# Softmax and its backward in parts between other steps, and score rows in another order, in an attention-and-FFN backward kernel

## The chip, the cores and the metric

The kernel runs on one core of a Trainium2 chip. The metric is the device time of one execution in microseconds (us). Before the change the median of three runs is 317.88 us (315.27 to 318.63). The profile below is of one more execution, with a span of 321.8 us from its first to its last instruction.

## What is computed

The forward pass is a layer norm, then grouped-query attention for one new token per batch entry plus a gated FFN, added to the input. The kernel returns the output and the gradients of eight inputs.

```python
B, Sq, D = 4, 1, 512;  Hq, Hkv, Sk, Dh = 32, 8, 4096, 128;  F = 1792
def _A_ref(x, k_cache, v_cache, wq, wo):
    W = min(4096, max(256, Sk // 4))              # 1024: only the last W keys are used
    rep = Hq // Hkv                               # 4 query heads for each key head
    q = (x @ wq).reshape(B, Sq, Hq, Dh).transpose(0, 2, 1, 3)
    k = jnp.repeat(k_cache[:, :, Sk - W:, :], rep, axis=1)
    v = jnp.repeat(v_cache[:, :, Sk - W:, :], rep, axis=1)
    p = _softmax(jnp.einsum("bhqd,bhkd->bhqk", q, k) * (Dh ** -0.5), axis=-1)
    o = jnp.einsum("bhqk,bhkd->bhqd", p, v)
    return o.transpose(0, 2, 1, 3).reshape(B, Sq, Hq * Dh) @ wo
def _B_ref(x, w_gate, w_up, w_down):
    return (_gelu(x @ w_gate) * (x @ w_up)) @ w_down
xn = _layernorm(A_x)
out = A_x + _A_ref(xn, A_k_cache, A_v_cache, A_wq, A_wo) + _B_ref(xn, B_w_gate, B_w_up, B_w_down)
# outputs: out and the gradients of A_x, k_cache, v_cache, wq, wo, w_gate, w_up, w_down, all bfloat16
```

The gradients of the two caches have the caches' full size (4 x 8 x 4096 x 128). Keys before the last 1024 take no part, so three quarters of both gradients are zeros, which the kernel writes from one tile of zeros (50 MB).

## The kernel before

The kernel first does the FFN and its backward, then the attention in four groups (t = 0 to 3) of two key heads. Matmuls run on TensorE (PE), evictions from PSUM on ScalarE (ACT) and VectorE (DVE), one masked copy of P, the masks and the stores' issue on GpSimd (POOL), loads on SyncE (SP). The zeros are issued from ACT's queue, at fixed places between its evictions.

Work that only feeds stores stands in a list `bg` of small pieces: one matmul and one eviction each; the last piece of a tile issues its store. `tick(n)` places the next n of them.

```python
    def tick(n):
        for _ in range(min(n, len(bg))):
            bg.popleft()()

    def scores(t, k):                     # k = 0: S = Q K^T;  k = 1: dP = dO V^T
        ...
        for g in range(GP):               # GP = 2 key heads
            for q in range(NQ):           # NQ = 4 quarters of the keys: 8 steps in all
                T_ps = ps_w.tile([P, JQ, P], BF16, name="T_ps", tag="w")
                for jj in range(JQ):      # 8 transposes
                    nc.tensor.transpose(T_ps[:, jj, :], blks[(t, g)][:, q * JQ + jj, :], ident[:])
                T_sb = tsb.tile([P, WQ, B], BF16, name="T_sb", tag="T", bufs=4)
                evac(T_sb..., T_ps..., 1024, half=True)              # on DVE
                for b in range(B):
                    nc.tensor.matmul(ps[b * RG:(b + 1) * RG, :], lhsT=..., rhs=T_sb[:, :, b], ...)
                tick(2)
                if q == 1:
                    zeros(4 if (g, k) != (0, 0) else 2 if t == NT - 1 else 0)

    def transposed(src, nm):
        pT_ps = ps_w.tile([P, JQ, P], BF16, name="pT_ps", tag="w")
        for jj in range(JQ):
            nc.tensor.transpose(pT_ps[:, jj, :], src[:, jj, :], ident[:])
        pT = attw.tile([P, JQ, P], BF16, name=nm, tag=nm, bufs=1)
        evac(pT[:].rearrange("p j (h b) -> p j b h", b=B),           # written in another order: PT, dST
             pT_ps[:].rearrange("p j (b h) -> p j b h", b=B), 1024, half=True)
        return pT[:].rearrange("p j (q g r) -> p j q g r", q=NQ, g=GP)

    def softmax(t):
        ...   # DVE: row maximum m;  PE: its transpose mT;  DVE: maximum over the quarters, negated
        ...   # PE: back to a column nm;  DVE: negm;  ACT: E_f = exp(S + negm), row sums es
        ...   # PE: es_ps, sums over the quarters;  DVE: rr = 1 / sum;  ACT: P_b = E_f * rr
        P_x = by_batch(P_b, "P_x", nc.gpsimd)                        # POOL: P spread by batch entry
        st[t].update(E=E_f, rr=rr, PT=transposed(P_x, "PT"), P=P_x)

    def softmax_d(t):
        ...   # DVE: gs = row sums of E_f * dP;  PE: gs_ps;  DVE: cc, Gt = (dP - cc) * E_f, dS_b
        dS_x = by_batch(dS_b, "dS_x", nc.vector)
        st[t].update(dST=transposed(dS_x, "dST"), dS=dS_x)

    def odq(t):                           # o from P^T and V, dq from dS^T and K
        for j in range(J):                # J = 32; four matmuls each, 16 rows of weights
            ...
                    nc.tensor.matmul(od_ps[r0:r0 + rep * B, :], lhsT=pT[:, j % JQ, j // JQ, g],
                                     rhs=blks[(t, g)][:, j, :], ...)
        ...   # od_r (DVE), its transpose od_T, and od_x, a masked copy on POOL

    # the pieces, each with its store through POOL:
    # dvdk(t, 0), dvdk(t, 1): 16 each (kv_ps; P_x or dS_x against the masks domr, qmr), 2 stores of 1 MB
    # dw(t): 8 dwo_ps and 8 dwq_ps from od_x, 4 stores of 0.5 MB (osb_o, osb_q; three buffers)

    # FFN backward: 14 iterations of transposes, eviction, matmuls, and tick(1)

        for t in range(NT):
            if t == 0:
                pre(t)                    # do and q of the group: woT steps, then wq; tick(2) a woT step
            masks(t)
            scores(t, 0)
            zeros(2 if t == 0 else 0)
            softmax(t)
            dvdk(t, 0)
            scores(t, 1)
            softmax_d(t)
            dvdk(t, 1)
            zeros(2 if t >= NT - 2 else 0)
            if t + 1 < NT:
                pre(t + 1)
            odq(t)
            fin(t)                        # sums for out and dx; four wqT steps with tick(2)
            load_next(t)                  # loads of group t + 2 into the buffers of group t
            dw(t)
        tick(len(bg))
        zeros(2 * B * G)                  # what is left of the zeros
```

The order in which the instructions of the loop stand on each engine is settled by a scheduler when the kernel is built; each engine then runs its own list in order.

Of the kernel before, what the change touches and what calls it, by code (L numbers as in the profile page):

```python
# [14 lines left out]
P = 128  # L15
# [3 lines left out]
def kernel(  # L19
# [94 lines left out]
    for eng, dst, src in ((nc.sync, dy_b, grad_out), (nc.scalar, x_b, A_x)):  # L114
# [18 lines left out]
    hmsk_f = const.tile([P, GP, rep * B], FP32, name="hmsk_f")  # L133
    idv = ident_f[:].rearrange("p (k g x) -> p k g x", k=2, g=GP)[:, :, :, 0:rep * B]
    nc.vector.tensor_tensor(out=hmsk_f[:], in0=idv[:, 0], in1=idv[:, 1], op=ALU.add)
    hmsk1 = const.tile([P, HG], FP32, name="hmsk1")
    nc.vector.reduce_sum(out=hmsk1[:], in_=hmsk_f[:].rearrange("p g (i b) -> p (g i) b", b=B), axis=AX.X)
    hmsk = const.tile([P, HG], BF16, name="hmsk")
    nc.vector.tensor_copy(out=hmsk[:], in_=hmsk1[:])
# [6 lines left out]
    rsum1 = const.tile([P, B, HG], FP32, name="rsum1")  # L146
    nc.vector.reduce_sum(out=rsum1[:].rearrange("p b h -> p (b h)"),
                         in_=ident_f[:].rearrange("p (b q h) -> p b h q", b=B, q=NQ), axis=AX.X)
    rsum = const.tile([P, B, NQ, HG], FP32, name="rsum")
    nc.vector.tensor_copy(out=rsum[:], in_=rsum1[:].unsqueeze(2).broadcast_to([P, B, NQ, HG]))  # L150

    msk_f = const.tile([P, GP, NQ], FP32, name="msk_f")
    nc.gpsimd.memset(msk_f[:], 1.0)
    for b in range(B):
        rs = slice(b * RG, (b + 1) * RG)
        nc.gpsimd.affine_select(out=msk_f[rs], in_=msk_f[rs], pattern=[[-rep, GP], [-HG, NQ]],
                                compare_op=ALU.is_ge, fill=0.0, base=0, channel_multiplier=1)
        nc.gpsimd.affine_select(out=msk_f[rs], in_=msk_f[rs], pattern=[[rep, GP], [HG, NQ]],
                                compare_op=ALU.is_ge, fill=0.0, base=rep - 1, channel_multiplier=-1)
    msk = const.tile([P, GP, NQ], BF16, name="msk")  # L160
    nc.vector.tensor_copy(out=msk[:], in_=msk_f[:])
# [12 lines left out]
    qm, dom = [const.tile([P, B, NS, RG + rep], BF16, name=nm) for nm in ("qm", "dom")]  # L174
# [56 lines left out]
    for dst, src, own, other in ((dyz, dy_b, slice(0, HP), slice(HP, P)), (xnz, xn_b, slice(HP, P), slice(0, HP))):  # L231
        nc.vector.tensor_copy(out=dst[own, :], in_=src[own, :])
        nc.vector.memset(dst[other, :], 0.0)
# [61 lines left out]
    def pre(t):  # L295

        wo_sb, wq_sb = wo_t[t], wq_t[t]
        dq_ps = ps_x.tile([P, 2, HG, B], FP32, name="doq_ps", tag="x")
        for h2 in range(HG // 2):
# [6 lines left out]
            for i in range(2):  # L306
                for c in range(ND):
                    nc.tensor.matmul(dq_ps[:, 0, 2 * h2 + i, :], lhsT=woT[:, i, c, :], rhs=dyT[:, c, :],
                                     start=(c == 0), stop=(c == ND - 1))
            tick(2)  # L310
        for h in range(HG):
            for c in range(ND):
                nc.tensor.matmul(dq_ps[:, 1, h, :], lhsT=wq_sb[:, c, h * Dh:(h + 1) * Dh], rhs=xnT[:, c, :],
                                 start=(c == 0), stop=(c == ND - 1))
        T4 = []
        for k, (sc, zt, nm) in enumerate(((None, dom, "do"), (scale, qm, "qs"))):
            xT4 = attw.tile([P, B, NQ, HG], BF16, name=nm + "T4", tag=nm + "T4")
            src = dq_ps[:, k].rearrange("p h b -> p b h").unsqueeze(2).broadcast_to([P, B, NQ, HG])
            if sc is None:
                nc.vector.tensor_copy(out=xT4[:], in_=src)  # L320
            else:
                nc.scalar.activation(out=xT4[:], in_=src, func=ACT.Copy, scale=sc)
            nc.vector.tensor_copy(out=zt[:, :, :, 0:rep].rearrange("p b s i -> p (b s) i"),
                                  in_=xT4[:].rearrange("p b q (g i) -> p (b q g) i", i=rep))
            T4.append(xT4)
        r_ps = ps_x.tile([P, 2, P], BF16, name="r_ps", tag="x")
        for k in range(2):
            nc.tensor.transpose(r_ps[:, k, :], T4[k][:].rearrange("p b q h -> p (b q h)"), ident[:])
# [4 lines left out]
    def masks(t):  # L333
        for k, nm in enumerate(("do", "q")):
            mr = attw.tile([P, GP, NQ, Dh], BF16, name=nm + "mr", tag=nm + "mr", bufs=1)
            nc.gpsimd.tensor_tensor(out=mr[:].rearrange("p g q d -> p (g q) d"),
                                    in0=st[t]["r4"][:, k, :].unsqueeze(1).broadcast_to([P, NS, Dh]),
                                    in1=msk[:].rearrange("p g q -> p (g q)").unsqueeze(2).broadcast_to([P, NS, Dh]),
                                    op=ALU.mult)
            st[t][nm] = mr  # L340

    def scores(t, k):

        lf = (qm, dom)[k][:].rearrange("p b s c -> p b (s c)")
        blks = (k_t, v_t)[k]
        ps = ps_a.tile([P, WQ], FP32, name="S_ps", tag=("S", "dP")[k])
        for g in range(GP):
            for q in range(NQ):
# [10 lines left out]
                tick(2)  # L359
# [12 lines left out]
    rsum_f = rsum[:].rearrange("p b q h -> p (b q h)")  # L372

    def transposed(src, nm):
# [5 lines left out]
        evac(pT[:].rearrange("p j (h b) -> p j b h", b=B), pT_ps[:].rearrange("p j (b h) -> p j b h", b=B), 1024, half=True)  # L380
        return pT[:].rearrange("p j (q g r) -> p j q g r", q=NQ, g=GP)

    def softmax(t):
        S = st[t]["S"]
        m = attw.tile([P, 1], FP32, name="m", tag="m")
        nc.vector.reduce_max(out=m[:], in_=S, axis=AX.X)
        mT_ps = ps_x.tile([1, P], FP32, name="mT_ps", tag="x")
        nc.tensor.transpose(mT_ps[:], m[:], ident_f[:])
        mx = attw.tile([1, B, HG], FP32, name="mx", tag="mx")
        nc.vector.reduce_max(out=mx[:].rearrange("o b h -> o (b h)"),  # L390
                             in_=mT_ps[:].rearrange("o (b q h) -> o b h q", b=B, q=NQ), axis=AX.X)
        mx4 = attw.tile([1, B, NQ, HG], FP32, name="mx4", tag="mx4")
        nc.vector.tensor_scalar(out=mx4[:], in0=mx[:].unsqueeze(2).broadcast_to([1, B, NQ, HG]), scalar1=-1.0,
                                scalar2=None, op0=ALU.mult)
        nm_ps = ps_x.tile([P, 1], FP32, name="nm_ps", tag="x")
        nc.tensor.matmul(nm_ps[:], lhsT=mx4[:].rearrange("o b q h -> o (b q h)"), rhs=one_f[:], start=True, stop=True)
        negm = attw.tile([P, 1], FP32, name="negm", tag="negm")
        nc.vector.tensor_copy(out=negm[:], in_=nm_ps[:])
        E_f = attw.tile([P, WQ], FP32, name="E_f", tag="E_f", bufs=1)
        es = attw.tile([P, 1], FP32, name="es", tag="es")  # L400
        nc.scalar.activation(out=E_f[:], in_=S, func=ACT.Exp, bias=negm[:, 0:1], scale=1.0, accum_out=es[:])
        es_ps = ps_x.tile([P, 1], FP32, name="es_ps", tag="x")
        nc.tensor.matmul(es_ps[:], lhsT=rsum_f, rhs=es[:], start=True, stop=True)
        rr = attw.tile([P, 1], FP32, name="rr", tag="rr")
        nc.vector.reciprocal(out=rr[:], in_=es_ps[:])
        P_b = attw.tile([P, WQ], BF16, name="P_b", tag="P_b", bufs=1)
        nc.scalar.activation(out=P_b[:], in_=E_f[:], func=ACT.Copy, scale=rr[:, 0:1])
        P_x = by_batch(P_b, "P_x", nc.gpsimd)
        st[t].update(E=E_f, rr=rr, PT=transposed(P_x, "PT"), P=P_x)

    def softmax_d(t):
        E_f, rr, dP = st[t]["E"], st[t]["rr"], st[t]["dP"]
# [346 lines left out]
```

## Time and profile before

| | before |
|---|---|
| median of three runs | 317.88 us |
| span of the profiled execution | 321.8 us |
| PE busy | 227.2 us (71%) |
| DVE busy | 169.5 us (53%) |
| ACT busy | 115.8 us (36%) |
| POOL busy | 67.7 us (21%) |
| moved by DMA | 112.38 MB (read 30.93 MB, written 81.01 MB) |

The busy time of an engine is the time in which it executes instructions, matmuls as the profile models their ends. "The span in 40 slices" gives the busy share of each engine in equal slices of 8.05 us, in tenths; PEclk is the clock granted to PE, in tenths of full speed, and DMA the mean busy share of the 16 DMA engines. In groups of instructions, a line gives the line of the code, engine, operation, output and input, count, then busy us and mean ns of one, then the idle time of the engine ahead of it and what ended most of that.

### The profile page before, as it was taken

What the parts mean: (1) busy time and instruction counts of PE and PEld (TensorE: products, weight loads), DVE (VectorE), ACT (ScalarE), POOL (GpSimd) and SP (SyncE); (2) the same over time, 40 slices, a digit from 0 to 9 for tenths busy, and PEclk for the clock granted to TensorE, in tenths of its full rate; (3) what the DMA queues carried; (4) which work ended last, traced back from release to release, by engine and by line L of the source; (5) the groups of instructions that cost most, each with busy time, mean ns of one, the idle gap of its engine ahead of it and who ended that gap; (6) DMA issues with size and microseconds to landing.
All of it is one profiled execution on the core that took longest, in us unless ns stands there. A gap on an engine that the chain in (4) does not pass through costs nothing.

```text
span 321.8 us, 6824 instructions
## 1 busy us (share of the span) xinstructions
PE 227.2 (71%) x2954; PEld 151.5 (47%) x2954; DVE 169.5 (53%) x312; ACT 115.8 (36%) x219; POOL 67.7 (21%) x80
## 2 busy tenths in 40 slices
PE   0769986938759894857499938647898487378710
PEld 0768863534437652534376514325664344354210
DVE  7763763526465573534546627263576254626760
ACT  2007752433423464214044622421455244017610
POOL 8200226130001433110033330000413300030400
PEclk9966997765967999577697978696899559558965
DMA  6999999999995799999639999999639969952895
GB/s 238 402 384 413 414 288 423 415 429 432 425 428 233 236 370 429 428 423 427 256 132 323 379 431 425 425 429 395 261 139 370 395 257 399 433 239 117 316 390 224
DMA packets 22013, 112.38 MB, mean 349 GB/s; under 512 B 1560, under 2 KB 7712, under 8 KB 13792
## 3 DMA queue, kind: packets, MB, share of 16 engines
q10 hardware_dynamic: 4624, 50.46, 37.3%
q1 hardware_dynamic: 11600, 30.81, 25.3%
q0 software_dynamic: 5760, 30.67, 24.3%
q8 instruction: 23, 0.38, 0.5%
q14 instruction: 6, 0.05, 0.0%
HBM read 30.93 MB, written 81.01 MB: 348 GB/s over the span
## 4 chain that ended last, share of the span: by engine, by line
PE 47%; DMA 23%; DVE 16%; issue 5%; ACT 4%; POOL 2%; ACTq 1%; SPq 0%; DVEq 0%; POOLq 0%
DMA out_dram<-osb_o 14%; PE kv_ps L461 9%; PE T_ps L351 8%; PE S_ps L356 4%; PE od_ps L434 4%; DMA out_dram<-osb_d 3%; PE wqT_ps L521 3%; DVE dST L96 3%; DMA out_dram<-osb_g 3%; DMA wd_sb<-in_B_w_down_dram 3%; PE acc_ps L196 3%; PE wgT_ps L656 2%; PE woT_ps L303 2%; DVE T_sb L96 2%; PE pT_ps L378 2%
## 5 line engine op out<-in xcount | busy, mean ns | idle before, releaser
L96 DVE COPY T_sb<-T_ps 128x1024 bf16<-128x1024 bf16 x64 | 44.3, 692 | 41.3 <-PE T_ps L351 41.0
L94 ACT CAST stg_dv<-kv_ps 128x512 bf16<-128x512 f32 x53 | 29.2, 588 | 67.6 <-PE kv_ps L461 67.1
L351 PE MATMUL T_ps<-ident,vb 128*128 128x128 bf16 x256 | 30.1, 273 | 7.9 <-DVE PT L96 3.3
L351 PEld LDWEIGHTS <-vb 128*128 128x128 bf16 x256 | 23.5, 125 | 21.3 <-issue 19.8
L94 ACT CAST stg_dk<-kv_ps 128x512 bf16<-128x512 f32 x46 | 25.3, 589 | 19.1 <-PE kv_ps L461 16.4
L461 PE MATMUL kv_ps<-domr,P_x 128*128 128x512 bf16 x64 | 25.7, 472 | 1.1 <-DVE wqT L96 1.1
L94 ACT CAST osb_q<-dwq_ps 128x512 bf16<-128x512 f32 x24 | 13.1, 590 | 36.0 <-PE dwq_ps L493 20.4
L351 PEld LDWEIGHTS <-kb 128*128 128x128 bf16 x256 | 18.6, 102 | 14.5 <-issue 9.2
L351 PE MATMUL T_ps<-ident,kb 128*128 128x128 bf16 x256 | 24.8, 228 | 0.5 <-ACT stg_dk L94 0.4
L461 PE MATMUL kv_ps<-qmr,dS_x 128*128 128x512 bf16 x64 | 21.1, 405 | 0.4
L94 ACT CAST osb_g<-dwg_ps 128x512 bf16<-128x512 f32 (+1 forms) x26 | 13.2, 557 | 21.6 <-PE dwg_ps L632 14.0
L446 POOL TENSOR_TENSOR od_x<-od_r,hmsk 128x1024 bf16<-128x1024 bf16 x4 | 7.5, 1882 | 54.3 <-DVE od_r L438 54.3
L96 DVE COPY PT<-pT_ps 128x1024 bf16<-128x1024 bf16 x4 | 9.7, 2434 | 14.9 <-PE pT_ps L378 14.9
L303 PE MATMUL woT_ps<-ident,wo_sb 128*128 128x128 bf16 x128 | 12.9, 252 | 5.8 <-DVE dST L96 5.8
L356 PE MATMUL S_ps<-T_sb,dom 128*32 128x256 bf16 x128 | 12.8, 390 | 6.0 <-DVE T_sb L96 5.8
L94 ACT CAST osb_o<-dwo_ps 128x512 bf16<-128x512 f32 x25 | 13.6, 588 | 8.7 <-PE dwo_ps L480 8.6
L96 DVE COPY woT<-woT_ps 128x1024 bf16<-128x1024 bf16 x16 | 11.1, 693 | 10.0 <-PE woT_ps L303 10.0
L96 DVE COPY wqT<-wqT_ps 128x1024 bf16<-128x1024 bf16 x16 | 11.0, 689 | 7.1 <-PE wqT_ps L521 7.1
L434 PE MATMUL od_ps<-kb,dST 128*16 128x128 bf16 x256 | 12.8, 281 | 2.5 <-DVE dST L96 2.5
L303 PEld LDWEIGHTS <-wo_sb 128*128 128x128 bf16 x128 | 10.3, 114 | 8.7 <-issue 7.9
L100 POOL DMA_DIRECT2D out_dram<-osb_q x8 | 5.8, 731 | 40.6 <-ACT osb_q L94 27.0
L356 PE MATMUL S_ps<-T_sb,qm 128*32 128x256 bf16 x128 | 12.7, 387 | 2.3 <-DVE T_sb L96 2.2
(194 smaller groups left out, 438.1 us busy)
## 6 DMA issues: line engine op xcount, KB each, us to landing
out_dram<-ztile ACTq DMA_DIRECT2D x8, 3072.0 KB, 16.0
out_dram<-ztile ACTq DMA_DIRECT2D x16, 1536.0 KB, 14.6
kb<-in_A_k_cache_dram SPq DMA_DIRECT2D x8, 1024.0 KB, 14.7
vb<-in_A_v_cache_dram SPq DMA_DIRECT2D x8, 1024.0 KB, 23.1
out_dram<-stg_dv POOLq DMA_DIRECT2D x8, 1024.0 KB, 5.9
out_dram<-stg_dk POOLq DMA_DIRECT2D x8, 1024.0 KB, 8.6
wo_sb<-in_A_wo_dram SPq DMA_DIRECT2D x4, 1024.0 KB, 6.8
wq_sb<-in_A_wq_dram SPq DMA_DIRECT2D x4, 1024.0 KB, 5.8
```

The lines of the kernel that those rows point to most:

```text
L94: last.append(nc.scalar.copy(out=out, in_=in_))
L96: return nc.vector.tensor_copy(out=out, in_=in_)
L196: nc.tensor.matmul(ps[:, c, :], lhsT=lf(c), rhs=rhs, start=(k == 0), stop=(k == len(terms) - 1))
L303: nc.tensor.transpose(wT_ps[:, i, c, :], wo_sb[:, 2 * h2 + i, c * P:(c + 1) * P], ident[:])
L351: nc.tensor.transpose(T_ps[:, jj, :], blks[(t, g)][:, q * JQ + jj, :], ident[:])
L356: nc.tensor.matmul(ps[b * RG:(b + 1) * RG, :], lhsT=lf[:, b, s * RG:(s + 1) * RG], rhs=T_sb[:, :, b], start=(g == 0 and q == 0), stop=(g = ...
L378: nc.tensor.transpose(pT_ps[:, jj, :], src[:, jj, :], ident[:])
L434: nc.tensor.matmul(od_ps[r0:r0 + rep * B, :], lhsT=pT[:, j % JQ, j // JQ, g], rhs=blks[(t, g)][:, j, :], start=(j == 0), stop=(j == J - 1) ...
L446: nc.gpsimd.tensor_tensor(out=X[:], in0=rows[:].unsqueeze(1).broadcast_to([P, HG, Dh]), in1=hmsk[:].unsqueeze(2).broadcast_to([P, HG, Dh]) ...
L461: nc.tensor.matmul(mps[:].rearrange("p q d -> p (q d)"), lhsT=src[:, jj, :], rhs=mr[:, g].rearrange("p q d -> p (q d)"), start=True, stop= ...
L521: nc.tensor.transpose(wT_ps[:, i, c, :], wq_sb[:, c, h * Dh:(h + 1) * Dh], ident[:])
L656: nc.tensor.transpose(wT_ps[:, i, c, :], wsb[:, c, fc * P:(fc + 1) * P], ident[:])
```

## The change

Three things are done.

1. A row of the scores was (batch, quarter, head) and becomes (batch, head in its key head, quarter, key head). The masks, the sums over quarters and the operands of the score matmuls follow. P^T and dS^T can then be copied from PSUM as they stand; the matmuls of `odq` pick their columns with a step of 8. The rows of `dyz` and `xnz` have to be put in the new order too, once, by a matmul with a selection matrix.
2. The softmax is cut into four parts, which are placed after steps 0, 1, 2 and 5 of the dP scores. Its backward is cut in two, placed after woT steps 0 and 2 of the next group's `pre`. The serial chains are meant to run beside other work of PE.
3. The background pieces are spread anew to fit: dV pieces begin within the dP scores, dK pieces within `pre`, all are placed before dW pieces are added, and the FFN backward takes two pieces an iteration instead of one.

```diff
-    def scores(t, k):
+    def scores(t, k, hooks):
 ...
-                tick(2)
+                for f in hooks.get(g * NQ + q, ()):
+                    f()
+                tick(2 if k or q % 2 else 1)
 ...
     def transposed(src, nm):
 ...
-        evac(pT[:].rearrange("p j (h b) -> p j b h", b=B), pT_ps[:].rearrange("p j (b h) -> p j b h", b=B), 1024, half=True)
-        return pT[:].rearrange("p j (q g r) -> p j q g r", q=NQ, g=GP)
+        evac(pT[:].rearrange("p j r -> p (j r)"), pT_ps[:].rearrange("p j r -> p (j r)"), 1024, half=True)
+        return pT
 ...
     def softmax(t):
         m = ...                                   # row maximum, at once
+        def a():  ...                             # mT, maximum over the quarters, mx4
+        def b():  ...                             # nm, negm, E_f and es
+        def c():  ...                             # es_ps, rr, P_b, P_x on POOL; then dvdk(t, 0)
+        def d():  u["PT"] = transposed(u["P"], "PT")
+        return {0: [a], 1: [b], 2: [c], 5: [d]}
 
     def softmax_d(t):
         Gt, gs = ...                              # row sums of E_f * dP, at once
+        def a():  ...                             # gs_ps, cc, Gt, dS_b, dS_x; then dvdk(t, 1)
+        def b():  u["dST"] = transposed(u["dS"], "dST")
+        return a, b
 ...
-                    nc.tensor.matmul(od_ps[r0:r0 + rep * B, :], lhsT=pT[:, j % JQ, j // JQ, g],
+                    nc.tensor.matmul(od_ps[r0:r0 + rep * B, :], lhsT=pT[:, j % JQ, (j // JQ) * GP + g:P:NS],
 ...
-            nc.gpsimd.tensor_tensor(out=mr[:]..., in0=r4 for 8 (g, q), in1=msk, op=ALU.mult)
+            for g in range(GP):
+                nc.gpsimd.tensor_tensor(out=mr[:, g], in0=r4 for 4 q, in1=msk[:, :, g]..., op=ALU.mult)
 ...
     def pre(t, hooks):                            # within the woT steps h2
-            tick(2)
+            for f in hooks.get(h2, ()):
+                f()
+            tick(3 if hooks else 2)
 ...
-        nc.vector.tensor_copy(out=dst[own, :], in_=src[own, :])          # dyz, xnz
+        nc.tensor.matmul(z_ps[own, :], lhsT=sel...[:, own], rhs=src[:], start=True, stop=True, ...)
+        nc.vector.tensor_copy(out=dst[own, :], in_=z_ps[own, :])
 ...
-            tick(1)                               # FFN backward
+            tick(2)
 ...
-            softmax(t)
-            dvdk(t, 0)
-            scores(t, 1)
-            softmax_d(t)
-            dvdk(t, 1)
+            scores(t, 1, softmax(t))
+            d1, d2 = softmax_d(t)
             zeros(2 if t >= NT - 2 else 0)
             if t + 1 < NT:
-                pre(t + 1)
+                pre(t + 1, {0: [d1], 2: [d2]})
+            else:
+                tick(2)
+                d1()
+                tick(6)
+                d2()
+                tick(2)
             odq(t)
             fin(t)
             load_next(t)
+            tick(len(bg))
             dw(t)
```

## The prediction

> **What bounds the kernel now.** I read the page first: the span in 40 slices and the DMA queues.
>
> ```profile
> PEclk9966997765967999577697978696899559558965
> DMA  6999999999995799999639999999639969952895
> GB/s 238 402 384 413 414 288 423 415 429 432 425 428 233 236 370 429 428 423 427 256 132 323 379 431 425 425 429 395 261 139 370 395 257 399 433 239 117 316 390 224
> ...
> q10 hardware_dynamic: 4624, 50.46, 37.3%
> q1 hardware_dynamic: 11600, 30.81, 25.3%
> q0 software_dynamic: 5760, 30.67, 24.3%
> ```
>
> Queue 10 carries the zeros, 1 the loads, 0 the stores. With 0.5% of instruction traffic the shares sum to 87.4% of 321.8 us, so 281 us of transfers: no order of the work goes below that without moving fewer bytes, and the change moves the same bytes. What can be won is the time in which the DMA engines have nothing to do. The digits show it: four dips (slices 12-13, 19-20, 28-29, 35-36), one for each of the four groups, plus the start, a small one at slice 32 and the tail.
>
> Next the stretches around these dips (columns: length; busy us and instructions of PE, PEld, DVE, ACT, POOL; granted PE clock; DMA share; GB/s):
>
> ```profile
> 96.00:104.00 8.00, 7.75 (x161) 5.86 (x164) 4.43 (x9) 2.52 (x5) 0.57 (x1) 0.71 0.54 228
> 104.00:112.00 8.00, 7.06 (x178) 5.32 (x163) 3.98 (x8) 3.64 (x7) 3.76 (x3) 1.00 0.75 251
> 152.00:156.00 4.00, 0.62 (x8) 0.51 (x9) 3.18 (x5) 0.00 (x0) 0.00 (x0) 0.91 0.99 419
> 156.00:168.00 12.00, 9.84 (x232) 7.46 (x232) 5.26 (x8) 3.91 (x7) 2.63 (x3) 0.75 0.31 127
> 220.00:240.00 20.00, 18.70 (x364) 13.75 (x352) 10.37 (x22) 9.10 (x17) 5.46 (x5) 0.83 0.57 234
> 256.00:264.00 8.00, 7.18 (x51) 4.14 (x48) 5.02 (x5) 2.83 (x5) 0.75 (x1) 0.50 0.64 255
> 284.00:300.00 16.00, 13.61 (x124) 7.59 (x123) 9.22 (x17) 8.93 (x16) 3.48 (x4) 0.76 0.38 154
> ```
>
> One minus the DMA share times the length gives idle DMA time: 3.7 + 2.0 in group 0, 8.3 in group 1, 8.6 in group 2, 2.9 and 9.9 in group 3. Those are 35.4 us. The same sum gives 2.7 at the start, 0.7 at 40-44, 0.8 at 240-256 and 3.7 after 316. In each dip PE is busy (9.8 of 12 us in 156-168): the queues ran dry behind compute that came too late. Between the dips the share is 1.0 and the engines wait for transfers instead.
>
> Why compute is late there, in the timeline of group 1:
>
> ```profile
> 151.08 0.42 DVE L415 CUSTOM_DVE_ANT_0 Gt<-E_f,S_ps 128x256 f32<-128x256 f32 x1 [0.61 <-ACT stg_dv L94]
> ...
> 154.37 0.62 PE L378 MATMUL pT_ps<-ident,dS_x 128*128 128x128 bf16 x8 [2.42 <-DVE dS_x L367]
> ...
> 155.03 2.42 DVE L96 COPY dST<-pT_ps 128x1024 bf16<-128x1024 bf16 x1 [0.71 <-PE pT_ps L378]
> 157.50 1.01 PE L303 MATMUL woT_ps<-ident,wo_sb 128*128 128x128 bf16 x8 [2.51 <-DVE dST L96]
> ```
>
> From 151.1 to 157.5 PE does a row sum and eight transposes. It waits 0.65, 2.42 and 2.51 us, 5.6 in all. The softmax ahead of it is alike: PE works 0.7 of the 5.1 us from the end of the transposed maximum (124.1) to P_x (129.2), and waits behind the 2.43 us copy PT afterwards.
>
> Last the groups and the waits:
>
> ```profile
> L96 DVE COPY T_sb<-T_ps 128x1024 bf16<-128x1024 bf16 x64 | 44.3, 692 | 41.3 <-PE T_ps L351 41.0
> L96 DVE COPY PT<-pT_ps 128x1024 bf16<-128x1024 bf16 x4 | 9.7, 2434 | 14.9 <-PE pT_ps L378 14.9
> L367 POOL TENSOR_TENSOR P_x<-P_b,bmsk 128x1024 bf16<-128x1024 bf16 x4 | 7.6, 1888 | 9.2 <-ACT P_b L407 9.2
> ...
> ACT osb_q L94 <- DMA out_dram<-osb_o: 15.5, 3, 6.5
> ```
>
> PT and T_sb are one shape and one size; the permuted writing costs 2434 against 692 ns. The last line is the reverse wait: compute held by the DMA, 6.5 us in group 1.
>
> **What the Trainium skill says.** "VectorE: DVE Perf Modes", section "What auto-detection actually checks": the doubled 16-bit mode needs step 1 in every tensor. The trace agrees: 2434 to 692 ns for PT and T_sb. "TensorE: Matmul & The Clock Gate", section "What's actually happening": the array falls to half clock after an idle window of about 3.4 us and comes back after a busy one. The trace agrees: clock 0.50 at 128-136 and at 256-264, each just after a softmax. "DMA: Bandwidth & Descriptors", section "Queues, rings and completion order": the DMA engines serve queues with work in turn. That fits a 0.5 MB osb_o store that took 20.06 us in the chain while loads and zeros were queued.
>
> **The change, part by part.** (a) Row order. PT and dST become plain copies: 8 x (2.43 - 0.69) = 13.9 us of DVE, each in a chain that PE waits for. Added: PE reads P^T columns with step 8 as weights in the od_ps loop (512 weight loads of 118 ns; their time with a step is not in the trace), two mask products of half size for one (1.89 us as before plus an overhead), and two selection matmuls at the start. (b) Softmax between the dP steps. In the built order of PE, transposes of V and dP matmuls now stand between the maximum, the exponential and the sum. Between the row sum es_ps and the first kv_ps there are in groups 1 to 3 only four short matmuls, so most of the reciprocal, P_b (0.51) and P_x (1.89) stays exposed: 129.2 - 126.4 = 2.8, less about 0.4, so 2.4 of 4.4 us. With 0.5 us of the row maximum and 2 us of the PT copy I put the gain at 4.5 us a group. (c) The backward between do steps: of 5.6 us I leave 1, so 4.6 us a group; in group 3 there are only dV and dK pieces to fill it, and I count half. (d) The pieces move earlier: dV starts within dP, dK is half done before od_ps, and the rest is flushed before dW. So dV and dK stores come out when the queues used to run dry. In POOL's order the second and later dV stores no longer stand behind od_x, which today waits 19.2 us for od_r (first dV store 164.97 in group 1). (e) The FFN loop takes two pieces an iteration: 14 more at about 0.4 us lengthen it by 5.6 us, taken off group 0 again.
>
> Middle group: period by the chain (last acc_ps 111.69 to 175.18) 63.5 us, less the DMA hold 6.5, less 9.1, gives 48 us of compute. In 112-176 the queues carry 22.18 MB in 86.9% of 64 us, that is 55.6 us. Transfers then become the bound. Counted from the first scores step of the group (my estimate from 12 us of scores, 17 of dP and 22 to the end of it), with the last zeros at +23 us, one dV store with them, one 8 us later and a dK store at +38, I get queues that last to about +51, and the next loads start near +44: no gap, or a short one.
>
> So I close: 4.8 of 5.7 us in group 0, 6.6 of 8.3, 7.0 of 9.4 in group 2 with 240-256, the 2.9 at 256-264, 5.0 of 9.9 in group 3, and the 0.7 at 40-44. Sum 27.0. Start and tail stay: the last zeros (3 MB) are still issued after the last eviction. From the median: 317.9 - 27.0 = 290.9, so 291 us.
>
> **The rivals.** First, transfers hide it: compute runs ahead, then waits longer for osb_o stores, and gaps only move. For it: the 15.5 us of that wait, and that P_b now stands in ACT's queue behind osb_q evictions which that wait holds. Against it: a gap arises only when queues are empty, and the bytes are the same. If half the gain is lost: 304. Second, PE's fixed order brings new waits (P_x on POOL at 1.89 us, dS_x behind evictions on DVE), or weights read with step 8 are slow: at twice 118 ns some 3 us a group. Then compute stays near 55 us a group, equal to the transfers, and about half the dips remain: 302. Third, all closes, with a PE that no longer falls to half clock: 281 of transfers plus 2.7 and 3.7 gives 287 in a profile of 321.8, some 283 on the scale of the median.
>
> **Range and chances.** 291 lies nearer to the third, since two of the four dips should close whatever PE's exact order is. The rivals together reach 307; the floor, 281. To stay within 2% (above 311.5) less than a quarter of the gain would have to arrive: faster 0.89, same 0.08, slower 0.03.
>
> **What would show it.** PT and dST at about 0.69 us; the four dips in the DMA line at 8 or 9 with only the last left; PE clock rarely at 5; the woT wait for dST gone, about 2.4 us of kv_ps on P_x left in each group; the sum of queue shares above 94%. Wrong if the od_ps loop grows beyond 3.5 us a group, if waits of osb_q on osb_o exceed 20 us, or if the dips stay although the serial chains are gone.

## The result, and the profile after

Beside each other on one chip the changed kernel takes 303.29 us (median of four, 298.58 to 307.03) and the kernel before 318.25 us. The ratio is 0.944, 95% interval 0.929 to 0.958. In some executions of either kernel the granted clock is lower and the time 1.5 to 3% longer; the ratios, here and below, leave these out, while the medians and the profile that follows (span 305.3 us) do not. By the ratio the change takes off 18 us, where 27 were predicted. 291 us was too low, and the range of 281 to 307 holds the result. A second profile of the same kernel, from the run e4_after, has a span of 297.4 us and is named where the two differ.

First the page of the changed kernel: the same three rows of the 40 slices (7.6 us each here), then the queues.

```profile
PEclk9996979959788999955987798559689997959955
DMA  7999963999999999999997699999990999999795
GB/s 228 397 379 419 420 262 129 334 421 418 431 426 430 421 400 406 426 425 424 430 423 268 222 380 431 423 427 406 419 381 30 392 404 411 414 411 385 267 395 211
...
q10 hardware_dynamic: 4624, 50.46, 39.5%
q1 hardware_dynamic: 11600, 30.81, 26.9%
q0 software_dynamic: 5760, 30.67, 24.9%
```

The shares with 0.5% of instruction traffic sum to 91.8% of 305.3 us, which is 280 us: the transfers are what they were (281). The time that went is time in which the DMA engines had nothing to do. One minus the DMA share, summed over stretches of 4 us, was 45.0 us before and is 30.1 us now (23.6 in the second profile). The span fell by 16.5 us, the idle time by 14.9, the transfers by 1. In the row of digits the dip of group 0 (slices 12-13 before) is gone and group 1's has become short (slices 21-22). Group 2's has stayed (slice 30, a 0), and a new one stands in slices 5-6.

The stretches behind these digits, columns as in the prediction:

```profile
40.00:44.00 4.00, 1.69 (x15) 1.41 (x15) 1.28 (x2) 1.89 (x4) 0.71 (x1) 0.74 0.63 249
44.00:48.00 4.00, 3.88 (x56) 2.84 (x54) 2.77 (x4) 2.27 (x5) 0.58 (x1) 0.83 0.20 70
48.00:52.00 4.00, 3.98 (x63) 2.91 (x61) 3.02 (x6) 2.58 (x6) 0.69 (x2) 1.00 0.56 229
52.00:56.00 4.00, 3.40 (x54) 2.26 (x51) 2.53 (x6) 2.62 (x5) 0.94 (x2) 1.00 0.65 161
96.00:112.00 16.00, 13.50 (x281) 9.96 (x282) 8.66 (x18) 5.72 (x11) 4.47 (x4) 0.89 1.01 422
126.00:133.00 7.00, 0.37 (x4) 0.09 (x2) 0.36 (x1) 0.34 (x1) 0.00 (x0) 0.84 1.02 430
133.00:140.00 7.00, 3.87 (x25) 2.33 (x25) 1.81 (x5) 2.73 (x7) 2.60 (x2) 0.50 1.02 427
188.00:192.00 4.00, 0.00 (x0) 0.00 (x0) 0.00 (x0) 0.00 (x0) 0.00 (x0) 0.59 1.00 421
224.00:236.00 12.00, 10.92 (x281) 8.31 (x278) 8.03 (x17) 4.67 (x10) 7.40 (x7) 1.00 0.39 156
280.00:288.00 8.00, 7.06 (x61) 3.17 (x59) 6.45 (x11) 5.88 (x11) 2.53 (x4) 1.00 0.69 276
```

Three things are to be seen. In 96-112, where group 0 had left 5.7 us idle, the share is 1.01. In 40-56 the queues are empty for 7.8 us while PE is busy. And in 126-133 and 188-192 the reverse holds: the queues are full and no engine works. Some 30 us later, in 224-236, the queues run dry behind PE, at full clock, for 7.3 us.

What the engines wait for in 126-133, in the timeline of the changed kernel (start, us, engine, and in brackets the wait ahead of it):

```profile
117.50 0.78 POOL L100 DMA_DIRECT2D out_dram<-osb_o  x1 [2.55 <-ACT osb_o L94]
...
132.66 0.59 ACT L94 CAST osb_q<-dwq_ps 128x512 bf16<-128x512 f32 x1 [9.34 <-DMA out_dram<-osb_o]
133.30 0.58 PE L524 MATMUL dwq_ps<-od_x,xnz 128*128 128x512 bf16 x1 [6.93 <-ACT osb_q L94]
...
195.90 0.59 ACT L94 CAST osb_q<-dwq_ps 128x512 bf16<-128x512 f32 x1 [12.44 <-DMA out_dram<-osb_o]
```

The dW tiles have three buffers. The fourth tile of a group, the second osb_q, needs the buffer of the first osb_o. The 0.5 MB store of that tile was issued at 117.50, and the eviction that waits for it starts at 132.66, 15 us later; loads and zeros are in the queues with it. In group 2 the same is 18 us (issue at 177.64, eviction at 195.90). The same wait before the change:

```profile
121.18 0.77 POOL L100 DMA_DIRECT2D out_dram<-osb_o  x1 [1.51 <-issue]
...
141.32 1.56 ACT L94 CAST osb_q<-dwq_ps 128x512 bf16<-128x512 f32 x3 [6.46 <-DMA out_dram<-osb_o]
```

The store took longer then, 20 us, and the wait was shorter. Before, ACT came to the eviction 13.7 us after the issue (141.32 - 6.46 - 121.18); after, 5.8 us after it (132.66 - 9.34 - 117.50).

The groups of the changed kernel that answer those of before (busy us, mean ns of one, idle time ahead):

```profile
L96 DVE COPY T_sb<-T_ps 128x1024 bf16<-128x1024 bf16 x64 | 43.9, 692 | 42.5 <-PE T_ps L358 42.1
L96 DVE COPY PT<-pT_ps 128x1024 bf16<-128x1024 bf16 x4 | 2.7, 681 | 0.0
```

and its waits (us in total, times, longest):

```profile
ACT osb_q L94 <- DMA out_dram<-osb_o: 25.1, 3, 12.4
DVE osb_q L96 <- DMA out_dram<-osb_o: 20.6, 3, 10.2
PE dwq_ps L524 <- ACT osb_q L94: 17.1, 3, 10.0
PE kv_ps L492 <- POOL P_x L376: 9.7, 4, 2.8
```

PT now costs what T_sb costs. The wait for the osb_o stores has grown from 15.5 us (6.5 the longest) to 25.1 (12.4). The wait of the woT step for dST, 5.8 us in three groups before, is not among the waits any more.

### The profile page after: what moved, and what is told of

The parts are those of the page before. It is cut to its first block, busy times and chain, and to the rows that moved or that the text cites. A ratio compares the mean times of both kernels' runs of the same rounds, so it can differ in the third digit from the quotient of the medians.

```text
span 305.3 us, 6840 instructions
## 1 busy us (share of the span) xinstructions
PE 217.9 (71%) x2956; PEld 142.4 (47%) x2956; DVE 156.0 (51%) x318; ACT 115.6 (38%) x219; POOL 67.2 (22%) x79
## 5 line engine op out<-in xcount | busy, mean ns | idle before, releaser
L492 PE MATMUL kv_ps<-qmr,dS_x 128*128 128x512 bf16 x64 | 24.2, 464 | 4.0 <-DVE dS_x L376 3.1
L358 PE MATMUL T_ps<-ident,vb 128*128 128x128 bf16 x256 | 26.0, 251 | 0.0
L358 PEld LDWEIGHTS <-vb 128*128 128x128 bf16 x256 | 20.1, 114 | 10.5 <-issue 8.8
L94 ACT CAST osb_q<-dwq_ps 128x512 bf16<-128x512 f32 x23 | 13.0, 589 | 30.6 <-DMA out_dram<-osb_o 25.1
L524 PE MATMUL dwq_ps<-od_x,xnz 128*128 128x512 bf16 x32 | 11.7, 395 | 17.3 <-ACT osb_q L94 17.1
L94 ACT CAST osb_o<-dwo_ps 128x512 bf16<-128x512 f32 x28 | 16.2, 587 | 10.0 <-PE dwo_ps L511 9.0
L94 ACT CAST osb_g<-dwg_ps 128x512 bf16<-128x512 f32 (+1 forms) x26 | 13.6, 555 | 15.6 <-PE dwg_ps L663 11.4
L363 PEld LDWEIGHTS <-dom 128*32 128x32 bf16 x128 | 4.8, 95 | 31.4 <-issue 29.8
L100 POOL DMA_DIRECT2D out_dram<-stg_dv x8 | 4.6, 578 | 57.6 <-ACT stg_dv L94 46.4
L96 DVE CAST osb_q<-dwq_ps 128x512 bf16<-128x512 f32 x9 | 6.1, 687 | 20.8 <-DMA out_dram<-osb_o 20.6
L96 DVE CAST stg_dk<-kv_ps 128x512 bf16<-128x512 f32 x17 | 11.7, 686 | 5.4 <-PE kv_ps L492 5.4
L96 DVE COPY wgT<-wgT_ps 128x1024 bf16<-128x1024 bf16 x14 | 9.7, 691 | 8.4 <-PE wgT_ps L687 8.4
## 6 DMA issues: line engine op xcount, KB each, us to landing
out_dram<-ztile ACTq DMA_DIRECT2D x16, 1536.0 KB, 16.5
vb<-in_A_v_cache_dram SPq DMA_DIRECT2D x8, 1024.0 KB, 25.1
```

Source lines behind the costliest of these rows:

```text
L94: last.append(nc.scalar.copy(out=out, in_=in_))
L96: return nc.vector.tensor_copy(out=out, in_=in_)
L100: d = eng.dma_start(out=out, in_=in_)
L363: nc.tensor.matmul(ps[b * RG:(b + 1) * RG, :], lhsT=lf[:, b, s * RG:(s + 1) * RG], rhs=T_sb[:, :, b], start=(g == 0 and q == 0), stop=(g = ...
L492: nc.tensor.matmul(mps[:].rearrange("p q d -> p (q d)"), lhsT=src[:, jj, :], rhs=mr[:, g].rearrange("p q d -> p (q d)"), start=True, stop= ...
L524: nc.tensor.matmul(mps[:], lhsT=xnz[:, c * P:(c + 1) * P], rhs=X[:, g * rep:(g + 1) * rep, :].rearrange("p i d -> p (i d)"), start=True, s ...
```

## The experiments

Ratios are to the kernel before on the same chip, with their 95% interval. e1 to e4 ran on one chip, e5 to e8 on another and e9 to e12 on a third. "The changed kernel" is e4 (0.944) in what follows, and a difference in us is taken at the 318 to 322 us of the kernel before.

### What the new gaps and waits cost

**e1: one piece an iteration of the FFN, as before.**

```diff
-            tick(2)                               # FFN backward
+            tick(1)
```

> The changed kernel with one piece an FFN iteration again (tick(1)); nothing else. Theory F (the FFN's second piece opened the gap of 7.9 us of idle DMA at 40-56 us: three osb_d buffers fill, evictions wait 5.3 and 5.1 us for their stores, the FFN ends 10 us later and with it the zeros and the loads of group 1): DMA share at 40-56 back to about 1, first zeros near 42 us instead of 52, time 5 to 7 us below the changed kernel, ratio to the kernel before near 0.925. Rival: the 14 pieces only move into group 0 and lengthen it by as much; gap gone but a new one at the end of group 0, time within 2 us of the changed kernel.

300.03 us, ratio 0.9438 (0.932 to 0.956); the changed kernel beside it took 302.23 us, 0.9442 (0.932 to 0.956). The same stretch in the profile of e1:

```profile
40.00:56.00 16.00, 11.58 (x185) 8.69 (x185) 7.74 (x15) 6.66 (x15) 6.97 (x9) 0.92 0.97 360
```

and its DMA row on the page:

```profile
DMA  6999999999999989999898899999991999999795
```

The gap behind the FFN closes, from some 7 us to 0.5, and the time stays the same. The other dips together grow from 16.7 us (second profile of the changed kernel) to 20.9. The 14 pieces that are not done in the FFN are done later. So this gap only showed work that was done early, and closing it alone is worth nothing measurable.

**e2: zeros of the S scores issued later.** In groups 0 to 2 the zeros that stand within the S scores go behind the next group's woT steps, so that loads, zeros and the osb_o store are not in the queues together.

```diff
-                if q == 1:
+                if q == 1 and (k or t == NT - 1):
                     zeros(...)
 ...
                 pre(t + 1, {0: [d1], 2: [d2]})
 ...
+            zeros(4 if t + 1 < NT else 0)
             odq(t)
```

> The changed kernel with the zeros that groups 0 to 2 issue within their S scores (3 MB in groups 1 and 2) issued after the next group's do steps instead, just before od_ps. Same bytes. Theory Q (the zeros and loads stand in the way of the osb_o stores, so osb_q evictions wait 25.1 us on ACT and 20.6 us on DVE in the whole run, and then the queues run dry at the group's end): waits of osb_q on osb_o under 15 us on ACT, dips at 164-176 and 224-236 (4.7 and 7.4 us idle) under 2 us each, time 7 to 10 us below the changed kernel. Rival C (the dips come from compute that is simply as long as the transfers): the waits shrink, the period of a middle group stays near 60 us, time within 3 us.

303.30 us, 0.948 (0.934 to 0.962). ACT's wait for osb_o falls from 24.3 us (e4) to 18.4, the longest from 11.3 to 6.7, and the time does not fall. Less than 15 us had been expected of the wait, so this shows that moving the zeros does not pay, and not that they have no part in it.

**e3: a fourth buffer for the dW tiles.** To make room, the normalized x in float32 is not kept but worked out again at the end.

```diff
-    outp = ctx.enter_context(tc.tile_pool(name="outp", bufs=3))
+    outp = ctx.enter_context(tc.tile_pool(name="outp", bufs=4))
```

> The changed kernel with four buffers instead of three for the osb tiles (room for it: the normalised input in fp32 is computed again at the end, one DVE instruction of about 0.5 us). Theory Q: the first osb_q eviction of the fourth tile no longer waits for the first osb_o store, 45.7 us of such waits fall under 10 us, PE runs on in the 7 and 10 us in which it stood still in groups 1 and 2, the dips shrink by about that, and the FFN's wait for osb_d goes too: 8 to 14 us below the changed kernel. Rival: the wait moves to the next store tile (stg_dv, osb_d of later rounds) and the time stays within 3 us, as the transfers are the bound anyway.

293.39 us, 0.920 (0.904 to 0.936): 2.5% less than the changed kernel, and its slowest execution (296.12 us) is faster than the fastest of e4 (299.18). The wait of osb_q for osb_o is gone from the list. What takes its place, in the waits of e3:

```profile
PE kv_ps L492 <- POOL P_x L376: 15.8, 4, 8.0
...
ACT P_b L424 <- DMA wo_sb<-in_A_wo_dram: 7.2, 1, 7.2
```

and in its timeline:

```profile
120.13 0.61 ACTq L100 DMA_DIRECT2D out_dram<-ztile  x1
...
122.19 0.16 DVE L422 RECIPROCAL rr<-es_ps 128x1 f32<-128x1 f32 x1
127.46 0.61 ACTq L100 DMA_DIRECT2D out_dram<-ztile  x1
128.19 0.51 ACT L424 ACTIVATE P_b<-E_f,rr 128x256 bf16<-128x256 f32 x1 [7.21 <-DMA wo_sb<-in_A_wo_dram]
```

Two zero stores stand one behind the other in ACT's own order, the second is issued 7.3 us after the first, and P_b, whose input has been ready since 122.4, stands behind it. The profile puts the wait down to a load, which P_b does not read. That it is the issue of the second store that is held up, with the queues full (DMA share 0.98 or more from 120 to 128), is read from the order and was not tried by itself.

**e4: the changed kernel once more**, for its own spread.

> The changed kernel itself on this chip, so that the three variants have it beside them: ratio to the kernel before 0.93 to 0.96, dips at 40-56, 164-176 and 224-236 us as in its first profile.

302.23 us, 0.944 (0.932 to 0.956). Idle DMA time 23.6 us: 6.9 in 40-56 again, 5.4 in group 2, 4.1 in group 3, and group 1's gap is shut. ACT waits 24.3 us for osb_o. The gap behind the FFN, the dip of group 2 and the waits are the kernel's; group 1's dip is not in every execution.

**e8: e1 and e3 together.**

> Both mends in one: four osb buffers and one piece an FFN iteration, else the changed kernel. If the FFN gap (4.9 us idle at 40-52 us with four buffers) and the store waits are separate losses: 286 to 290 us, ratio to the kernel before about 0.905. If the transfers take it up: 292 to 294, as with four buffers alone (293.4).

292.85 us, 0.917 (0.905 to 0.929). From the page of e8:

```profile
DMA  6999999999999999999999999999984999999795
...
q10 hardware_dynamic: 4624, 50.46, 42.0%
q1 hardware_dynamic: 11600, 30.81, 27.8%
q0 software_dynamic: 5760, 30.67, 26.7%
```

The shares now sum to 97.0% of a span of 287.4 us, 279 us, and 13.6 us are idle: this is the picture that the prediction drew for the change alone, its third rival's 287 us in a profile. In time e8 is not told apart from e3.

**e10: the fourth buffer in the kernel before**, with the edit of e3 and nothing else.

> The kernel before with a fourth buffer for the dW tiles (the normalized x in float32 is worked out anew at the end to make room), nothing else. In the changed kernel the fourth buffer was worth about 2.4%. Theory S (the change turned late compute into waits for the stores of osb_o, so the fourth buffer pays only together with it): here it removes the 15.5 us of ACT's wait for osb_o, but the dips are behind compute that the softmax holds, so the time moves by 1% at most, ratio 0.99 to 1.005. Rival (three buffers held the kernel before as much, and half of the changed kernel's later gain has nothing to do with the change): ratio 0.97 to 0.98.

313.35 us, 0.980 (0.971 to 0.990). My theory said 1% at most and falls: three buffers held the kernel before as well, by 2.0%. With the fourth buffer in both kernels the ratio of the change is 0.9201/0.9801 = 0.939, without it 0.944, and the intervals of these are wider than their difference. So the wait costs both kernels about the same: the change neither brought this cost nor took it away.

### What the parts of the change are worth

**e5: a permuted copy again, written with a step of 16.** PT and dST are written so that the 16 weight columns of a matmul lie side by side. As the operands stand in the edit, PSUM is read in order, and successive elements are written 16 elements apart.

```diff
-        evac(pT[:].rearrange("p j r -> p (j r)"), pT_ps[:].rearrange("p j r -> p (j r)"), 1024, half=True)
+        evac(pT[:].rearrange("p j (s x) -> p j x s", s=NS), pT_ps[:].rearrange("p j (x s) -> p j x s", s=NS), 1024, half=True)
 ...
-    lhsT=pT[:, j % JQ, (j // JQ) * GP + g:P:NS]
+    lhsT=pT[:, j % JQ, ((j // JQ) * GP + g) * BI:((j // JQ) * GP + g + 1) * BI]
```

> The changed kernel, but PT and dST are written in a permuted order again (columns grouped by quarter and key head, so that od_ps reads its 16 weight columns side by side); everything else as changed. Theory D (the plain copy is worth what lies in a chain: 8 x 1.74 us of DVE, dST before od_ps and PT ahead of the T_sb copies): PT and dST 2.4 us each, DVE busy up by 14 us, time 4 to 8 us above the changed kernel (302.2). Theory Q' (the middle groups are held by stores and zeros, and DVE has room; PE waits for neither copy now that other work stands between): time within 3 us of the changed kernel, 14 us of DVE notwithstanding.

338.68 us, 1.062 (1.052 to 1.073): slower than the kernel before. The copies are larger than I had taken them for, as the groups of e5 show:

```profile
L96 DVE COPY PT<-pT_ps 128x1024 bf16<-128x1024 bf16 x4 | 17.8, 4459 | 0.0
L96 DVE COPY dST<-pT_ps 128x1024 bf16<-128x1024 bf16 x4 | 17.8, 4456 | 0.5 <-PE pT_ps L387 0.5
```

and its waits:

```profile
PE T_ps L358 <- DVE PT L96: 11.8, 4, 3.0
PE kv_ps L492 <- DVE dST L96: 7.9, 3, 3.1
```

8 x (4.46 - 0.69) = 30 us more of DVE made 35 us more of time than the changed kernel (0.944 of 321.65 is 303.7). PE waits for the copy PT in every group although the chains are interleaved: the transposes of a later dP step (T_ps) start only when it is done.

**e9: a permuted copy, written with a step of 8**, meant to have the 2.43 us of before.

```diff
-        evac(pT[:].rearrange("p j r -> p (j r)"), pT_ps[:].rearrange("p j r -> p (j r)"), 1024, half=True)
-        return pT
+        pv = pT[:].rearrange("p j r -> p (j r)").rearrange("p (r j) -> p j r", j=JQ)
+        evac(pv, pT_ps[:], 1024, half=True)
+        return pv
```

> The changed kernel, but PT and dST are written again with a step of 8 elements and read from PSUM as they stand, as the kernel before did with a step of 4; the od_ps loop takes its weights with a step of 64. The question is what the permuted copy costs at the size it had before. If a step in what is written costs what it did before (2.43 us against 0.69), DVE has 14 us more, 3.5 us a group. Theory D (the copies lie on the path of PE, as the run with 4.46 us copies says): most of the 14 us come back, 9 to 15 us more than the changed kernel, ratio 0.975 to 0.995. Theory H (a copy of 2.4 us is hidden beside the dP steps and the next woT steps, and only one of 4.5 us is not): within 4 us of the changed kernel, ratio 0.94 to 0.957. LDWEIGHTS of the od_ps loop stay near 107 to 140 ns.

337.50 us, 1.058 (1.049 to 1.067). Both expectations missed, again by the size of the copy. The group of e9:

```profile
L96 DVE COPY PT<-pT_ps 128x1024 bf16<-128x1024 bf16 x4 | 18.8, 4697 | 0.0
```

and the wait behind it:

```profile
PE T_ps L358 <- DVE PT L96: 12.8, 4, 3.2
```

So the step of the writing counts: 0.69 us as it stands, 2.43 with a step of 4 elements (before), 4.70 with 8 (e9), 4.46 with 16 (e5); all of them read PSUM in order. The doubled mode, by which the prediction explained the 2434 and 692 ns, can give a factor of 2 and not the 3.5 between them. The Trainium skill, "SBUF — State Buffer", section "Door 1: The DMA port swizzle (why `[64,N]` ≈ `[32,N]`)", speaks of lines of 16 bytes, each of which must be hit at least twice for full bandwidth. The trace agrees in part: with a step of 4 bf16 elements (8 bytes) two writes fall in a line, with 8 (16 bytes) or 16 (32 bytes) one, and the copy nearly doubles from 4 to 8 and grows no further to 16. But the same note counts steps up to 8 bf16 as free, and there the 4.70 us decide against it; why a step of 4 already costs 2.43 us is not shown. Per us of copy, e5 and e9 lost 1.16 and 1.12 us of time. Carried back to 2.43 us that would be about 16 us for the eight copies. It is an estimate along a straight line, and rather too high, as e11 shows below; the copy with a step of 4 was not tried in the changed kernel.

**e6 and e7: one chain in one piece again.** In e6 the four parts of the softmax run ahead of the dP steps; in e7 the two parts of its backward run ahead of the next group's woT steps, in groups 0 to 2.

```diff
-            scores(t, 1, softmax(t))              # e6
+            for fs in softmax(t).values():
+                for f in fs:
+                    f()
+            scores(t, 1, {})
 ...
-                pre(t + 1, {0: [d1], 2: [d2]})    # e7
+                d1()
+                d2()
+                pre(t + 1, {9: []})               # no hook, tick(3) kept
```

> The changed kernel with the four parts of the softmax one after the other ahead of the dP scores again (P pieces wait in the list from there); backward still in parts. Theory S (the chain that PE waited for is the gain): 4 groups at 4 to 5 us, PE idle between mT and P_x back at about 4.4 us a group, time 8 to 15 us above the changed kernel. Rival Q (compute that comes earlier only waits longer for the osb_o stores): the waits of osb_q on osb_o fall to the 15 us of the kernel before, time within 4 us of the changed kernel.

> The changed kernel with both parts of the softmax backward ahead of the next group's do steps again (three pieces a do step as changed). Theory S: this chain lies after the last zeros of a group, where the queues run dry, so each of the 3 groups loses its 4 to 5 us in full, dips at the ends of groups 0 to 2 come back or grow, time 10 to 15 us above the changed kernel. Rival: dV and dK stores that now come early keep the queues fed, time within 4 us.

e6: 307.86 us, 0.965 (0.956 to 0.975). e7: 305.24 us, 0.959 (0.952 to 0.965). Against 0.944 that is about 7 and 4.6 us, each between its two expectations; the interval of e7 overlaps that of the changed kernel, so its 4.6 us are weakly shown. The waits of e6:

```profile
PE pT_ps L387 <- POOL P_x L376: 11.4, 4, 2.9
...
ACT osb_q L94 <- DMA out_dram<-osb_o: 12.4, 2, 9.0
DVE osb_q L96 <- DMA out_dram<-osb_o: 3.4, 1, 3.4
```

The serial chain brings its wait of 2.9 us a group back, and at the same time the wait for osb_o is half or less of what it is with the interleaved softmax (24.3 and 16.3 us in e4). So part of what the interleaving gains is paid back as a longer wait for the stores.

**e11: both chains in one piece**, the edits of e6 and e7 together.

> The changed kernel with both chains in one piece again: the softmax's four parts ahead of the dP steps, the backward's two ahead of the next group's woT steps. Left of the change are the row order with its plain copies, and the new places of the background pieces. Alone, the forward chain was worth about 2.1% and the backward one about 1.5%. If the two add up: ratio 0.978 to 0.985. If they stand in for each other (both only feed the same wait for stores): 0.965 to 0.97. If everything lies in the interleaving and the row order is worth nothing: 0.995 or more. The dips of the DMA line should be back in groups 1 to 3.

306.41 us, 0.964 (0.957 to 0.970). With both chains serial the kernel is as fast as with one of them serial (e6 0.965, e7 0.959). So neither interleaving alone is worth anything that can be measured; the gain comes only when both are there, and a serial chain of either kind loses most or all of it. What is left, the row order with plain copies and the new places of the pieces, is worth 3.6%, 11.6 us. Both interleavings together add 2.0%, some 6 us. The dips of the DMA row, expected back in groups 1 to 3, are in groups 0, 2 and 3 (3.8, 6.2 and 5.2 us), beside the gap behind the FFN:

```profile
DMA  7999964999999869999999999999974997998795
```

### A version that is faster than both

**e12: e8, and the zeros left at the end (3 MB) issued ahead of the last group's od_ps loop.**

```diff
                 d2()
                 tick(2)
+                zeros(2 * B * G)
             odq(t)
```

> The changed kernel with one FFN piece an iteration, a fourth buffer for the dW tiles, and the zeros that are left at the end (3 MB) issued ahead of the last group's od_ps loop instead of after the last eviction. The first two alone gave a ratio of 0.917. Theory T (the queues run dry for some 3 to 4 us around 284 since the last zeros and stores come late, and bytes at hand there fill it): the dip in the last group goes, 287 to 291 us, ratio 0.900 to 0.910. Rival (the end is set by the last dW store, which these zeros then delay, or the zeros at the end were only filling time in which the last stores run anyway): no change, 0.915 to 0.92, or slower.

292.58 us, 0.911 (0.903 to 0.919): 8.9% less than the kernel before. Against e8 (0.905 to 0.929) the further step is not told apart, and the value lies between the two expectations. The idle stretch of 1.6 us at 264-272 in e8 is not in the profile of e12, but one of 11.7 us stands in group 2, at 204-228, where e8 has 4.8. From the waits of e12:

```profile
ACT stg_dv L94 <- DMA kb<-in_A_k_cache_dram: 20.2, 2, 16.0
```

stg_dv does not read kb; as with P_b in e3, each of these evictions stands behind a zero store in ACT's order, and the longer one ends just ahead of the stretch. In e8 these waits are 15.6 us. They are the longest of ACT that the profile puts down to DMA in e8 and e12, and nothing was tried against them. The fourth buffer is the step that pays.

## Why the prediction was right, and where not

**(a) Copies and row order: right.** DVE fell from 169.5 to 156.0 us, 13.5 for the 13.9 worked out. That copies at this place lie on the path of PE is what e5 and e9 showed most clearly, with larger ones, and e11 puts the part of the change that holds them at 11.6 us, two thirds of the whole. The fear of the second rival, weights read with a step of 8, is settled by the trace. At the least a weight load takes 105 ns against 85 before, and the od_ps matmul beside it 219 in both. e5, with the columns side by side, has 85 again, and e9, with a step of 64, has 104 to 105.

**(b) Softmax: waits right, worth too high.** 2.4 us of kv_ps waiting for P_x were left, as worked out (9.7 us in four groups). Of the 4.5 us a group, 2 were the copy; for the remaining 2.5, 10 us in all, e6 measured about 7, with the backward interleaved. With a serial backward, e7 against e11, it is 0.5% or 1.6 us and not told from nothing.

**(c) Backward: right in the trace, worth less.** The woT wait is gone, and of kv_ps waiting for dS_x 3.1 us in all are left, about 1 us a group. The 4.6 us a group hold 1.7 of the copy, so nearly 3 were to come from the new place, some 10 us with group 3 at half. e7 measured 4.6 us, and e11 none on top of a serial softmax. The two were counted one by one in the prediction, and neither pays without the other.

**The step that failed is "less the DMA hold 6.5 ... Transfers then become the bound".** I took the hold out of the compute of the middle group as if it were slack that goes when compute is faster. It is a wait for one buffer. It ends when a 0.5 MB store has landed in full queues (20 us after its issue before the change, 15 and 18 after it), and compute that comes to the buffer sooner waits longer: 6.5 us became 9.3 and 12.4. In it PE stands idle for 6.9 us, and after it the clock granted is 0.50 in 133-140, as the Trainium skill, "TensorE: Matmul & The Clock Gate", section "What's actually happening", has it for PE after an idle window. What follows starts late; in e3, without the wait, the dip of group 2 is 2.6 us. So the sums for groups 1 and 2, 6.6 and 7.0 us to be closed, came out as 3.6 and about 2 in the first profile. The second has group 1 shut and 5.4 us left in group 2. This is the first rival (304 us), which I had put at half the gain and judged less likely since "the bytes are the same". The sign named for it, more than 20 us of osb_q waiting for osb_o, came: 25.1.

Removing the wait is worth 2.5% (e3), and was worth 2.0% before as well (e10). So it is not a loss that the change brought; it is a cost of both kernels whose end the prediction had booked to the change. With the 6.5 us left in, its own sum is 63.5 - 9.1 = 54.4 us of compute against 55.6 of transfers, which is the case for which it put 302. And the kernel in which the wait is gone, e3, has 0.920, near the 0.915 (290.9 of 317.9) of the prediction. As an estimate from e10 (2.0%, 6.4 us) and from e3 (0.944 to 0.920, 7.7 us), 6 to 8 of the 9 missing us are this step.

**(e) The FFN: wrong, but without weight.** 5.6 us longer had been predicted, and the loads behind it start 10.3 us later (51.6 after 41.3). The other 4.7 us are PE waiting there for an osb_d eviction, which the store before it held for 5.3. So at 40-44, where 0.7 us were to close, 7.8 opened up to 56. e1 took this back and gained nothing.

**Groups 0 and 3: better than said.** Group 0 closed wholly (5.7 for 4.8), the stretch at 256-264 too (2.9). Group 3 has 2.5 us left in the first profile and 4.1 in the second, for 4.9 expected. Half clock is rarer (mean granted clock 0.79 before, 0.84 and 0.86 in the two profiles after); in the last group's dip it is 1.00 after (280-288) against 0.76 before (284-300). That the clock is the reason was not tried.

**What stays open.** The parts do not sum to a budget: e11's 11.6 us and the 6 us of the interleavings make the 18, but how much of the 11.6 is the copies and how much the new places of the pieces was not separated. Nor was it tried whether the interleavings are worth more once the fourth buffer is there, or what it brings to keep ACT's evictions from standing behind zero stores.

## What to carry to other kernels

A wait for a store's buffer is not slack: before counting on a faster chain, look for the buffer that compute will reach sooner, and compare its number with the time that a store takes in full queues. Gaps of the DMA engines are symptoms and do not add up: close one alone, as e1 did, and it may open again elsewhere. A layout that spares a strided copy may be worth as much as interleaving, when the engine that copies is also the one that every step of the loop needs: here the part of the change with the layout made 3.6%, both interleavings 2.0%. And what two interleavings are worth is only known when each of them, and both, have been taken out.

## What was not expected of the hardware

- A copy of 128x1024 bf16 from PSUM on DVE takes 0.69 us as it stands, 2.43 with a step of 4 elements in what is written, 4.70 with 8 and 4.46 with 16 (in this order: the changed kernel, the kernel before, e9, e5).
- Weight columns with a step of 8 elements cost a load of 16 columns 105 ns against 85 at the least, with a step of 64 no more (e9), and the matmul stays at 219.
- With the queues full (DMA share 0.98 or more), the second of two zero stores on ACT was issued 7.3 us after the first, and what stood behind it in ACT's order waited (e3).
